# Mask products on GpSimd, quarter-array bias products and a new order of work in a fused attention and mixer kernel

## The chip, the core and the metric

The kernel runs on one core of a Trainium2 chip. A core has several engines that run side by side, each with its own queue: TensorE multiplies matrices (PE in the profile; its weight loads are PEld), VectorE (DVE) and ScalarE (ACT) work on elements, GpSimd (POOL) can do so too and issues transfers, and SyncE (SP) issues transfers. They wait for each other by semaphores. The metric is the device time of one execution in microseconds, as the median of several runs.

## What is computed

Attention over 4 images, 8 heads, 768 tokens and 64 numbers per head, in which a query sees 8 global keys and the last 96 tokens, with a bias that falls with the distance; then a mixer over the 512 numbers of each token.

```python
scores = scale * np.matmul(q, k.transpose(0, 1, 3, 2))
dist = np.where(is_global & ~is_local, float(n_local), np.abs(rel))
scores = np.where(keep, scores - slopes[:, None, None] * dist, -1e9)
a = np.exp(scores - max);  a = a / a.sum(-1)
x = np.matmul(a, v)                      # (4, 768, 512) after the heads are joined
xt = x.transpose(0, 2, 1)
u = x + (xt @ U @ V).transpose(0, 2, 1)  # rank 32, over the tokens
out = u + np.maximum(u @ w_ch1, 0.0) @ w_ch2   # 512 -> 2048 -> 512
```

Inputs and output are float32; the kernel multiplies in float16.

## The kernel before

**Staging.** Heads are taken in pairs, so there are 16 pairs p, four to an image. Everything is kept in SBUF; the eight PSUM banks (`ps`) take the products. q and k of a pair are loaded by GpSimd's queue and cast on the way (`lq`, `lk`; `add_load`, L491 to L547). There are two forms of load: pairs below `BP` are loaded by token, one transfer with long rows (L502), and the others by two transfers with rows of one head (L506). Pair 0 alone comes as float32 by SP's queue and is cast by ACT or VectorE (`Ck0`, `Cq0`, L413 and L411). q and k then have to be turned so that the head's numbers lie on the partitions: either by TensorE (`TK`, `TQ`; by-token loads with half-array products, `tr`, L629, others with full ones, `flip`, L648) and a copy out of PSUM (`EK`, `EQ`), or, for pairs in `QD`, by a transposing transfer on SP (L662).

**Attention.** A pair has three score groups s of two query blocks each. For the pairs of image 0 the bias and the mask come first as a product of a scaled identity `ib` with a table of distances `rel3` (`SB`, L758), and the scores are added to it in PSUM (`S`, L777, 64 rows to a product, two heads side by side). ACT takes the exponential (`EX`, L842). For the other images the exponential is multiplied by a precomputed factor instead (`MK`, L851 and L855, on VectorE, inputs `ep` and `mask`). Then come the product with v (`PV`, L912 and L913), the reciprocal of the sum and the normalizing (`RC`, `NM`, L951).

**Mixer.** The rank-32 part runs through `UP`, `XU`, `HM` (L896, L1025, L1007) and a sum into `uT` (`E0`, L1084, VectorE, which reads PSUM). The first big product, u times w_ch1, is done in eight units z for an image: either plainly (`M1a`, `M1b` with a relu on ACT, L1121 and L1145) or with seven products in place of eight (Strassen's way; `ZP1` to `ZP7`, L1215), whose partial sums ACT copies out of PSUM (`ZU`, `ZW`, `ZX`, L411) and VectorE adds (`ZA`, `ZB`, `ZD`, L1232). Before the change image 0 is plain, image 1 takes units 2 to 7 this way, images 2 and 3 all eight: 22. The second product is also done with seven (`RS`, L1310, and `P1` to `P7`, L1321), from sums of relu's results that VectorE makes (`Sa` to `Sd`, L1277), and VectorE adds the results to x (`DA` to `DH`, L1333, L1352, L1365). SP stores the rows (`O`, L1374).

**What sets the order.** Each step above is a named task. The list `ORDER` gives the order of all tasks by hand; a planner (L142) walks the list, gives out PSUM banks and buffers, estimates a start for each task by constants of its own, and the tasks are emitted by that start. So the order on each engine is fixed when the program is built, an engine does its tasks strictly one after the other, and a task that waits holds those behind it. `CFG` says by letter (A, D, P, S) which engine takes a copy of each pair. At the end of the kernel, `idle` (L1406) puts products of zeros into TensorE's queue: seven wide ones ahead of the first real product, and narrow ones into planned gaps of the first stretch.

Of the kernel before, what the change touches and what calls it, by code (L numbers as in the profile page):

```python
# [11 lines left out]
FP16 = mybir.dt.float16  # L12
I32 = mybir.dt.int32
AF = mybir.ActivationFunctionType
ALU = mybir.AluOpType
# [6 lines left out]
wz lk1 lk0 lq0 iota ones0 lk2 relf lq1 rel3 Ck0.1 Ck0.0 bias0 lv0 TK0 Cq0.1 Cq0.0 bias1 SB0.2 SB0.0 SB0.1 TQ0 EK0.1  # L22
lq2 EK0.0 KO0.1 bias2 mask0 bias4 EQ0.0 KO0.0 EQ0.1 TK1 EK1 S0.0 S0.2 S0.1 TQ1 EX0.0 mask4 TK2 SB1.2 KO1 EX0.1 SB1.1
ones1 EQ1 S1.2 lk3 lv1 VC0 VG0 EK2 EX0.2 S1.1 PV0 mask6 EX1.2 lq3 SB1.0 TQ2 ones3 TK3 EX1.1 EQ2 S1.0 RC0 NM0 KO2 VC1
VG1 ones2 vs1 lv2 vs0 SB2.0 SB2.2 S2.2 S2.0 EX1.0 TQ3 PV1 lv3 back XC0 EQ3 u16 w1_0 VC2 EX2.2 RC1 EK3 EX2.0 VG2 KO3
SB2.1 S2.1 NM1 VC3 XC1 SB3.1 SB3.0 S3.0 S3.1 EX2.1 EX3.0 PV2 mixl SB3.2 S3.2 EX3.1 RC2 NM2 VG3 EX3.2 XC2 UP0 UP1 XE1
lk4 PV3.0 PV3.1 XU1 lk5 PV3.2 TE1 HM1 E01 E00 RC3.0 RC3.2 TK4 RC3.1 NH3.0 NH3.2 NH3.1 UP2 UP3.0 UP3.1 UP3.2 EK4 w1_1
TK5 NM3 XE3 M1a0.0 XU3 TE3 mask2 EK5 M1c0.0 HM3 E03 w1_3 vz lq4 w1_2 w1_5 E13 M1a0.3 M1c0.3 M1a0.2 M1c0.2 E02 M1d0.2
M1d0.3 M1b0.2 M1d0.0 M1b0.0 M1b0.3 TQ4 RL0.2 RL0.0 KO4 M1a0.1 M1c0.1 M1d0.1 M1b0.1 RL0.3 EQ4 M1b0.4 M1a0.7 RL0.1 RM0.4
mask1 S4.1 RL0.7 S4.0 EX4.2 M1b0.5 M1b0.7 lv4 EX4.1 EX4.0 RM0.5 M1a0.5 M1a0.4 RL0.5 mask5 M1a0.6 M1b0.6 w1_4 RM0.6  # L30
RL0.6 RM0.7 mask3 lk7 lk6 w1_7 w1_6 w2_3 M1a0.15 MK4.2 TK6 vs2 w2_1 lq5 TK7 EK6 KO6 MK4.1 VC4 VG4 MK4.0 PV4 lq7 lq6
w2_2 lv5 w2_0 M1a0.10 M1b0.12 RL0.10 ZS1 RL0.4 M1a0.13 RL0.13 RM0.12 RC4 M1a0.9 NM4 TD0 Sa0.0 Sb0.0 KO5 Sc0.0 EK7
Sd0.0 TWa1 TWb1 M1b0.9 M1b0.15 M1b0.8 RM0.9 mask7 RL0.9 RL0.15 M1b0.13 M1b0.10 RM0.15 TQ5 EQ5 RM0.13 M1b0.11 RM0.8
RM0.11 M1b0.14 M1a0.12 M1a0.14 ZS2 RM0.10 RL0.12 RL0.14 RM0.14 M1a0.8 M1a0.11 RL0.8 RL0.11 lq8 lv6 S5.0 lk11 lv9 S5.1
lk10 Sa0.1 Sb0.1 EX5.0 lk8 RS0.1 Sd0.1 P20.1 lv7 EX5.1 TQ6 TQ7 MK5.1 MK5.0 TWa0 RS0.2 P20.2 P30.2 VC5 EQ7 EX5.2 EQ6
VG5 P10.1 S6.1 P50.1 P10.2 MK5.2 TWb0 DA0.1 KO7 DA0.2 EX6.2 PV5 EX6.1 S6.0 VC6 DF0.2 P60.2 EX6.0 VG6 RC5 NM5 XC5 XT5
EQ8 MK6.0 XC4 XT4 P30.1 S7.1 EX7.2 MK6.2 MK6.1 Sc0.1 DF0.1 EX7.1 P60.1 P50.2 PV6 S7.0 DB0.2 EX7.0 RS0.0 P10.0 UP5 UP4
RC6 DB0.1 MK7.1 P70.2 P20.0 MK7.0 NM6 MK7.2 VC7 VG7 DC0.2 PV7 DD0.2 P70.1 DA0.0 RC7 NM7 XC6 XE5 XU5 ZS3 P40.2 TE5
DG0.2 HM5 P60.0 DB0.0 XC7 P30.0 UP6 UP7 P50.0 VC9 XE7 XU7 EK8 E05 E04 DD0.1 EK10 TE7 DF0.0 XT6 XT7 P70.0 lk15 lq9 lq12
HM7 E06 DD0.0 E07 E17 ZT1 P40.1 ZP11.7 lk9 ZP11.6 M1a1.1 ZP21.7 M1b1.1 RL1.1 ZP11.4 P40.0 ZU1.6 ZP21.6 ZU1.4 ZP61.6  # L40
ZW1.6 lv8 DG0.0 lv10 ZU1.7 ZA1.6 DC0.0 ZP21.4 lq10 ZP61.4 ZP51.6 ZP71.6 ZP11.5 ZW1.4 ZP71.4 ZA1.4 KO8 ZA1.7 DG0.1
DC0.1 ZX1.6 ZX1.4 ZB1.6 ZP51.4 EQ12 M1b1.4 ZP61.7 ZP41.6 ZB1.4 ZU1.5 ZP21.5 ZP31.6 ZP41.4 ZP61.5 ZA1.5 KO10 ZR1.6
ZD1.6 ZP31.4 ZD1.4 O0.3 ZW1.7 O0.2 RM1.4 ZP71.7 ZR1.4 S8.1 ZW1.5 ZX1.7 ZP51.7 ZP71.5 ZP41.7 ZP51.5 ZB1.7 EX8.2 ZP31.7
ZX1.5 ZP41.5 ZB1.5 TD1 S8.0 ZP31.5 EX8.1 ZP11.3 ZR1.7 ZP11.2 EK9 EX8.0 ZP21.3 ZU1.3 ZD1.7 ZU1.2 ZR1.5 VC8 ZP21.2
M1a1.0 ZP61.2 MK8.2 MK8.1 ZD1.5 MK8.0 O0.5 EQ10 M1b1.0 ZP61.3 ZP51.3 ZW1.2 ZP51.2 O0.4 O0.1 O0.0 EQ9 Sa1.1 lk12 ZA1.3
# [1414 lines left out]
```

## Time and profile before

| what | value |
|---|---|
| median of 3 runs | 212.17 us (212.1 to 213.61) |
| profiled execution | 213.81 us, its span 211.9 us |
| TensorE busy | 204.9 us, 97% |
| VectorE busy | 180.5 us, 85% |
| ScalarE busy | 139.2 us, 66% |
| GpSimd busy | 74.2 us, 35% |
| moved by transfers | 27.40 MB |

The span runs from the first to the last instruction; some 1.9 us of the execution lie around it. Busy times are sums of an engine's instructions; a matrix product's duration contains its way through the array, so that a following product starts before the first has ended. A row of the groups names the line, the engine, the operation, the tiles (out<-in), the shape and count, then the busy time, the mean duration in ns, and the idle time just before with what ended it.

### The profile page before, as it was taken

The page shows a single profiled execution, that of the slowest core. Times are in us where ns is not written, and L with a number is a line of the kernel's source. Part 1 is how long each engine was busy: PE and PEld are TensorE (multiplying, and loading weights), DVE is VectorE, ACT ScalarE, POOL GpSimd, SP SyncE. Part 2 cuts the span into 40 slices and gives each one's busy share as a digit, 9 for nine tenths or more (in the row PEclk, how much of TensorE's full clock was granted, in tenths as well). Part 3 has the DMA queues.
Part 4 walks back from the last instruction along what each step waited for, and adds up shares of the span by engine and source line. Part 5 has one row for each costly group of instructions (what it writes and reads, how often), then busy time and mean ns, then how long its engine had stood idle before and what let it go on. Part 6 is the DMA issues. An engine that isn't in the chain of part 4 may idle for free.

```text
span 211.9 us, 5673 instructions
## 1 busy us (share of the span) xinstructions
PE 204.9 (97%) x2281; PEld 149.1 (70%) x2281; DVE 180.5 (85%) x369; ACT 139.2 (66%) x254; POOL 74.2 (35%) x98
## 2 busy tenths in 40 slices
PE   5999899999999999999999999999999999999992
PEld 1665756666888876556889866567889766668892
DVE  4389841999999999799999999899999996899872
ACT  4599869998999617899976366778783258740000
POOL 7699797647910494082755000003000000000000
PEclk9999999999999999999999999999999999999999
DMA  6999999999995899999999983866603110000644
GB/s 181 170 161 159 162 183 175 208 169 191 158 115 100 120 161 146 204 267 148 113 140 136 135 178 66 210 175 52 67 0 77 37 49 3 2 0 3 223 152 175
DMA packets 103643, 27.40 MB, mean 129 GB/s; under 512 B 91584, under 2 KB 100736, under 8 KB 103616
## 3 DMA queue, kind: packets, MB, share of 16 engines
q0 software_dynamic: 72192, 13.59, 83.7%
q1 hardware_dynamic: 31424, 13.45, 30.0%
q8 instruction: 18, 0.29, 0.6%
q14 instruction: 9, 0.07, 0.1%
HBM read 27.75 MB, written 6.29 MB: 161 GB/s over the span
## 4 chain that ended last, share of the span: by engine, by line
PE 86%; DVE 4%; DMA 3%; POOL 2%; issue 2%; POOLq 0%
PE ps L1321 36%; PE ps L1215 24%; PE ps L1121 6%; PE ps L777 5%; DMA w<-in_moe_w_ch_dram 3%; PE ps L758 3%; PE ps L913 3%; PE ps L912 2%; PE ps L1310 1%; PE ps L1145 1%; PE ps L648 1%; PE ps L629 1%; PE ps L896 1%; POOL stgk L506 1%; PE ps L1007 1%
## 5 line engine op out<-in xcount | busy, mean ns | idle before, releaser
L842 ACT ACTIVATE ep<-ps 128x1024 f16<-128x1024 f32 (+1 forms) x48 | 44.0, 955 | 6.9 <-PE ps L777 6.6
L1321 PEld LDWEIGHTS <-htr 128*128 128x128 f16 x392 | 35.8, 98 | 5.8 <-issue 0.5
L1321 PEld LDWEIGHTS <-sA 128*128 128x128 f16 x288 | 27.3, 98 | 4.2 <-issue 0.3
L506 POOL DMA_DIRECT2D stgk<-in_k_dram x24 | 20.2, 859 | 26.8 <-DMA kT<-stgk 26.7
L1333 DVE TENSOR_TENSOR x_sb<-x_sb,ps 128x256 f32<-128x256 f32 (+1 forms) x60 | 26.8, 463 | 3.1 <-PE ps L1321 2.6
L1232 DVE CUSTOM_DVE_ANT_0 htr<-ps,zu 128x384 f16<-128x384 f32 x50 | 26.0, 549 | 3.7 <-PE ps L1215 3.0
L411 ACT ACTIVATE zu<-ps 128x384 f32<-128x384 f32 x50 | 22.9, 497 | 6.6 <-PE ps L1215 4.4
L1215 PEld LDWEIGHTS <-w 128*128 128x128 f16 x176 | 17.0, 98 | 10.5
L1321 PE MATMUL ps<-w,sA 128*128 128x256 f16 x192 | 24.3, 273 | 0.0
L1321 PE MATMUL ps<-tB,htr 128*128 128x256 f16 (+1 forms) x200 | 24.1, 268 | 0.1
L1321 PE MATMUL ps<-w,htr 128*128 128x256 f16 x192 | 24.0, 273 | 0.0
L506 POOL DMA_DIRECT2D stgq<-in_q_dram x24 | 20.1, 860 | 2.9 <-PE ps L648 2.1
L1121 PE MATMUL ps<-uT,w 128*128 128x384 f16 x112 | 19.5, 326 | 0.0
L510 POOL DMA_DIRECT2D vt<-in_v_dram x16 | 16.6, 1043 | 7.5 <-ACT vo L411 3.7
L855 DVE TENSOR_TENSOR ep<-ep,mask 128x1024 f16<-128x1024 f16 x24 | 16.0, 682 | 3.6 <-ACT ep L842 3.6
L1215 PE MATMUL ps<-zt,w 128*128 128x384 f16 x88 | 19.0, 326 | 0.0
L1215 PE MATMUL ps<-uT,w 128*128 128x384 f16 x88 | 18.5, 326 | 0.0
L1121 PEld LDWEIGHTS <-w 128*128 128x128 f16 x112 | 10.8, 98 | 7.0
L951 DVE TENSOR_TENSOR x_sb<-ps,rcp 128x768 f32<-128x768 f32 x16 | 15.2, 952 | 0.3
L1215 PE MATMUL ps<-zt,zs 128*128 128x384 f16 x64 | 14.5, 326 | 0.0
L777 PE MATMUL ps<-qT,kT 64*128 64x128 f16 x192 | 14.1, 218 | 0.0
L913 PE MATMUL ps<-vt,ep 128*128 128x65 f16 x192 | 13.4, 193 | 0.3 <-DVE ep L851 0.3
(124 smaller groups left out, 397.8 us busy)
## 6 DMA issues: line engine op xcount, KB each, us to landing
out_dram<-x_sb SPq DMA_DIRECT2D x22, 256.0 KB, 2.6
vt<-in_v_dram POOLq DMA_DIRECT2D x16, 192.0 KB, 6.1
stgk<-in_k_dram POOLq DMA_DIRECT2D x24, 96.0 KB, 6.3
stgq<-in_q_dram POOLq DMA_DIRECT2D x24, 96.0 KB, 6.5
w<-in_moe_w_ch_dram POOLq DMA_DIRECT2D x8, 256.0 KB, 7.5
w<-in_moe_w_ch_dram POOLq DMA_DIRECT2D x4, 512.0 KB, 8.8
stgk<-in_k_dram POOLq DMA_DIRECT2D x3, 192.0 KB, 5.2
stgq<-in_q_dram POOLq DMA_DIRECT2D x3, 192.0 KB, 5.4
```

What stands on the lines that cost most here:

```text
L411: nc.scalar.activation(dst, src, AF.Copy)
L506: nc.gpsimd.dma_start(o[:, i], src[b, h0 + i].rearrange("(n p) d -> p n d", p=P))
L510: nc.gpsimd.dma_start(vt[gv.slot][:, :, :, 0:D], v[b, h0:h0 + 2].rearrange("h (n p) d -> p h n d", p=P),)
L777: nc.tensor.matmul(t[:, hi, j * P:(j + 1) * P], lhs, qt[r, i * P:(i + 1) * P], start=not biased, stop=True, skip_group_check=biased,)
L842: nc.scalar.activation(ep[gep.slot][:, :, lo:512], ps[:, gsc.slot:gsc.slot + 2, lo:512], AF.Exp, scale=qk_scale)
L855: nc.vector.tensor_tensor(ev, ev, mv, ALU.mult)
L913: nc.tensor.matmul(o, e[:, hi, (j + 1) * P:(j + 2) * P], vv[:, hi, i, 0:D1], start=(i == 0), stop=True)
L1121: nc.tensor.matmul(ps[:, g.slot, 0:HS], w1[:, dc, jt * P:(jt + 1) * P], ub[:, dc, i * HS:(i + 1) * HS], start=(dc == 0), stop=(dc == NDC - 1),
L1215: nc.tensor.matmul(bank(g), a()[:, i], bq[:, i], start=first and i == 0, stop=last and i == 1, skip_group_check=True,)
L1232: return lambda: nc.vector._custom_dve(TENSOR_ADD_SAT, out=o, in0=x(), in1=y(), s0=3.0e38, s1=0.0)
L1321: nc.tensor.matmul(o if part is None else o[:, part], a[:, j, c0 + cols.start:c0 + cols.stop], bq[:, j] if part is None else bq[:, j, part ...
L1333: nc.vector.tensor_tensor(o, o, x, ALU.add)
```

## The change

The same result is computed. The parts:

- Twelve of the 36 mask products (all of pair 8, one or two of pairs 9, 11, 12, 13, 14 and 15) run on GpSimd instead of VectorE.
- The bias products of pairs 1 to 3 are each split into two products of 64 rows and 64 columns (the scaled identity's off-diagonal blocks are zero). The two heads use opposite row halves, for which a copy of `rel3` with swapped halves (`rel3s`) is made, so that four products cover the four quarters of the array.
- Pairs 4 to 6 are now loaded by token (and turned by half-array products); pair 7 joins the pairs whose q and k are turned by transfers, nine in all.
- Image 1 takes all eight units of the first product with seven products: 24 units.
- For nine pairs the sum into `uT` no longer reads PSUM: ACT copies (`AH`) and VectorE adds in SBUF.
- Single copies change engines (`CFG`'s letters): both halves of pair 0's k are cast by ACT, two bias scalings go to VectorE, three pairs' values are copied by SP, one cast is no longer a transfer.
- Nine wide products of zeros lead instead of seven, and the narrow ones number 25 instead of 10.
- `ORDER` is new throughout. The planner's constants change, which tells in the emitted order and the count of zeros alone. A wider VectorE sum (`DX`) is added, with no pair that uses it, and an unused branch for `KG` goes.

```diff
-    "Z": [[1, [2, 3, 4, 5, 6, 7]], ...
+    "Z": [[1, [0, 1, 2, 3, 4, 5, 6, 7]], ...
-    "BP": 4,
+    "BP": 7,
-    "IB": "AAAA",  "C0": "ADDDDADA",
+    "IB": "AADD",  "C0": "AADDDADA",
-    "VO": "DDDDDAAAAAAADASA",  "XC": "DDADAAAAAAAAQAAA",
+    "VO": "DDDDDDAAASSADSDA",  "XC": "DDADAAAAAADAAAAA",
-    "QD": [8, 9, 10, 11, 12, 13, 14, 15],
-    "EA": (),
+    "QD": (7, 8, 9, 10, 11, 12, 13, 14, 15),
+    "EA": [4, 5, 6, 8, 9, 10, 12, 13, 14],
+    "SBQ": [1, 2, 3],
+    "MP": [24, 25, 26, 27, 35, 36, 38, 40, 43, 44, 45, 47],
...
+    def swap_rel():
+        for i in range(2):
+            nc.vector.tensor_copy(rel3s[64 * i:64 * i + 64], rel3[64 - 64 * i:128 - 64 * i])
...
                 for hi in range(2):
-                    bb = rel3[:, 128:384].unsqueeze(1).broadcast_to((P, 2, 256)) if s else rel3
-                    nc.tensor.matmul(t[:, hi, lo:512], ib[:, h0 + hi], bb, start=not by_glob, stop=by_glob, skip_group_check=True)
+                    if not quads:
+                        nc.tensor.matmul(t[:, hi, lo:512], ib[:, h0 + hi], cols(rel3, slice(0, P)), start=True, stop=False, skip_group_check=True)
+                        continue
+                    for i in range(2):
+                        o, r = slice(64 * i, 64 * i + 64), slice(64 * (i ^ hi), 64 * (i ^ hi) + 64)
+                        nc.tensor.matmul(
+                            t[o, hi, lo:512], ib[r, h0 + hi, r], cols(rel3s if hi else rel3, r), start=True, stop=False, skip_group_check=True,
+                        )
...
+            slow = 3 * p + s in CFG.get("MP", ())
+
-            def mk(s=s, gep=gep):
+            def mk(s=s, gep=gep, eng=nc.gpsimd if slow else nc.vector):
                 e = ep[gep.slot]
                 if s == 0:
-                    nc.vector.tensor_tensor(e[:, :, 128:512], e[:, :, 128:512], mask[:, h0:h0 + 2], ALU.mult)
+                    eng.tensor_tensor(e[:, :, 128:512], e[:, :, 128:512], mask[:, h0:h0 + 2], ALU.mult)
...
-    done, until = c_wz.end + 0.3, pl.names["M1a0.0"].start
+    done, until = 0.0, pl.names["M1a0.0"].start
...
+                bank = pl.unused("ps", done, t.start)
+                if not done:
+                    idle(9, 512, bank)
+                    done = pl.READY - 0.1
                 gap = t.start - done
-                bank = pl.unused("ps", done, t.start)
-                if bank is not None and done < 5.0:
-                    idle(int(gap / 0.43 + 0.6), 512, bank)
-                elif bank is not None and gap > 0.15:
+                if bank is not None and gap > 0.15:
                     idle(int((gap - 0.05) / 0.056), P, bank)
```

`AH` and its sum are in the kernel before already, unused (`EA` was empty):

```python
nc.scalar.activation(zu[gh.slot].bitcast(FP16)..., ps[:, gx.slot:gx.slot + 2, 0:HS], AF.Copy)   # AH
nc.vector.tensor_tensor(o, o, zu[gh.slot].bitcast(FP16), ALU.add)                             # E0, o = uT[b % 2][:, hp]
```

More of the change, by code (lines that the diff above doesn't have):

```diff
@@ L204, in run @@
             raise RuntimeError("order and tasks differ")
-        clock = {PE: 0.0, ACT: 2.0, DVE: 0.7, POOL: 0.75, SP: 0.7}
+        clock = {PE: self.READY, ACT: 2.0, DVE: 0.7, POOL: 0.75, SP: 0.7}
         last = {}
@@ L208, in run @@
         mode = 0
-        dma_free = {POOL: 0.0}
+        dma_free = {POOL: 0.0, SP: 0.0}
         shared_port = {POOL: [], DVE: []}
@@ L860, in attention @@
                 MK = add(
-                    DVE, 0.57 if s == 0 else 0.7, mk,
+                    POOL if slow else DVE, ((0.57, 0.7), (1.8, 2.35))[slow][s > 0], mk,
                     [EX, c_mask[h0], c_mask[h0 + 1]], fast=2, name=f"MK{p}.{s}",
```

207 lines of the change are left out of this document (111 added, 96 removed).

## The prediction

> **What bounds the kernel now.** I read the page first, then stretches of the span, then the chain, then the start by itself.
>
> ```profile
> span 211.9 us, 5673 instructions
> ...
> PE 204.9 (97%) x2281; PEld 149.1 (70%) x2281; DVE 180.5 (85%) x369; ACT 139.2 (66%) x254; POOL 74.2 (35%) x98
> ```
>
> ```profile
> 0.00:5.33 5.33, 3.17 (x7) 0.91 (x8) 2.46 (x12) 2.21 (x4) 4.27 (x12) 1.00 0.67 180
> 5.33:42.00 36.67, 35.52 (x476) 23.20 (x477) 22.81 (x57) 30.53 (x51) 30.20 (x41) 1.00 1.74 173
> 42.00:188.80 146.80, 146.78 (x1604) 107.87 (x1604) 138.53 (x265) 106.25 (x200) 39.75 (x46) 1.00 1.14 117
> ...
> 144.00:168.00 24.00, 24.00 (x343) 20.01 (x342) 23.41 (x42) 15.12 (x23) 1.83 (x2) 1.00 0.41 52
> ```
>
> After each stretch and its length stand the busy times of PE, PEld, DVE, ACT and POOL. From 42 us on, TensorE is busy for 146.78 of 146.80 us: there the time is the number of products, each at its own pitch, and nothing else. Two things qualify that. VectorE is busy 138.5 of the same 146.8 us, and 23.4 of 24 us while the last image's attention runs: it is the next bound. And up to 42 us TensorE has gaps (5.33 us until real work, 1.15 us after) and, as the start shows below, products at half pace. So I price three things: the products, the first 10 us, and whether anything makes TensorE wait after 42 us.
>
> **The products.** The chain gives the pitch of each kind (start, length, count), free of the drain that a product's own duration contains.
>
> ```profile
> 14.59 0.33 PE ps L758 x2
> 14.92 0.85 PE ps L629 x24
> ...
> 19.39 0.86 PE ps L758 x4
> ...
> 48.56 0.34 PE ps L648 x6
> ...
> 61.81 1.85 PE ps L1321 x16
> 63.66 0.55 PE ps L777 x16
> 64.21 1.85 PE ps L1321 x16
> ...
> 171.90 16.93 PE ps L1215 x104
> ...
> 189.60 17.16 PE ps L1321 x160
> ```
>
> So 384 columns take 0.163 us (16.93/104; a bias product 0.165), 512 take 0.215, 256 take 0.107, 128 take 0.057. Half-array products run two at a time: 24 of 128 columns took 0.85, against 12 x 0.057 = 0.68. A change of array shape costs time too: 16 score products (half the rows, two at a time) should take 16 x 0.028 = 0.45 and took 0.55; the 16 full products behind them should take 16 x 0.107 = 1.72 and took 1.85. That is about 0.12 per change of shape.
>
> 1. Bias products of pairs 1 to 3. Eighteen go (6 of 384, 12 of 512 columns: 6 x 0.165 + 12 x 0.215 = 3.57 us); 36 quarter-array ones come, in nine groups of four that cover the four quarters. No row here shows quarters. Halves run two at a time, by rows and by columns, so I take four at a time: 3 x 0.165 + 6 x 0.215 = 1.79. Net -1.78. Bounds: two at a time 0.0; one at a time +3.57; no gain beyond four, since the four columns' streams are the same length.
> 2. Units 0 and 1 of image 1 take 14 products instead of 16: -4 x 0.163 = -0.65. They add six ACT copies, six VectorE adds (row L1232 below, 0.549 each: +3.3 us) and two ACT relus against fewer relus; bounded with VectorE's account below.
> 3. Transposes. Pairs 4 to 6 turn by half-array products instead of full ones and pair 7 by the DMA queue: 48 full ones of 128 columns go (-2.74), 72 halves come (+2.02): -0.72. Pair 7's two DMA turns stand in SP's queue long before its scores: in the built order some 15 us of products lie between, and a turn lands in 3.4 us (row below). Nothing waits for it.
> 4. Changes of shape, counted in the built order: 77 before, 89 after, 12 x 0.12 = +1.44.
>
> Sum of the products: -1.78 - 0.65 - 0.72 + 1.44 = **-1.71 us**, on the path in full, because TensorE has no idle time to swallow it.
>
> **The start.**
>
> ```profile
> 0.89 3.17 PE L1408 MATMUL ps<-zero 128*128 128x512 f16 x7 [0.89 <-POOL zero L428]
> ...
> 3.79 0.52 ACT L411 ACTIVATE stgk<-sA 128x384 f16<-128x384 f32 x1 [1.77 <-DMA sA<-in_k_dram]
> ...
> 4.38 0.80 DVE L413 CAST stgk<-sA 128x384 f16<-128x384 f32 x1
> ...
> 5.33 0.80 PE L648 MATMUL ps<-ident,stgk 128*128 128x128 f16 x6 [1.27 <-DVE stgk L413]
> ...
> 5.73 0.63 DVE L413 CAST stgq<-sA 128x384 f16<-128x384 f32 x2 [0.54 <-DMA sA<-in_q_dram]
> ...
> 5.92 2.55 PE L758 MATMUL ps<-rel,ibe 128*128 128x512 f16 x6
> ...
> 8.27 0.85 PE L648 MATMUL ps<-ident,stgq 128*128 128x128 f16 x6
> 9.15 0.56 DVE L413 COPY qT<-ps 128x384 f16<-128x384 f16 x1 [2.80 <-PE ps L648]
> ...
> 9.83 0.29 PE L777 MATMUL ps<-qT,kT 64*128 64x128 f16 x2
> ...
> 11.63 0.50 PE L629 MATMUL ps<-ident,stgk 128*64 128x128 f16 x12
> ```
>
> Six bias products took 2.55 us where six at the later pitch would take 1.2 (4 x 0.215 + 2 x 0.165) and a drain of 0.2: until about 10 us TensorE runs at half its pace, although the granted clock prints 1.00 there. The seven products of zeros end at 4.06 and TensorE then idles 1.27 us, waiting for the half of k that VectorE casts behind its mask building (4.38 to 5.18). In the changed kernel ACT casts both halves (3.79 + 2 x 0.52 = 4.83, so TensorE starts near 4.95), and nine wide and five narrow products of zeros (9 x 0.43 + 5 x 0.107 = 4.4 us from 0.89) leave no pause. Then comes q's transpose: before, it stood behind the six bias products and started at 8.27 although q was cast at 6.36; now it starts at about 6.5, and 8.27 to 9.83 = 1.56 us later, at 8.1, the first scores can run. Two thirds of the bias products now stand between: behind a transpose at half pace (6.5 + 0.64) they take 1.5 at half pace (to 8.6) or 0.76 at full pace (to 7.9). So the first scores come 1.2 to 1.75 us earlier; I take **-1.4 us**. Bounds: 0 if ACT, busy 30.5 of 36.7 us here, holds the next stages; -2.2 if the clock is full throughout. ACT loses two bias scalings and the odd copy, so I lean to the gain.
>
> [...]
>
> **The mask products, and who waits.**
>
> ```profile
> L1232 DVE CUSTOM_DVE_ANT_0 htr<-ps,zu 128x384 f16<-128x384 f32 x50 | 26.0, 549 | 3.7 <-PE ps L1215 3.0 <-ACT zu L411 0.6 <-ACT htr L1260 0.2
> ...
> L855 DVE TENSOR_TENSOR ep<-ep,mask 128x1024 f16<-128x1024 f16 x24 | 16.0, 682 | 3.6 <-ACT ep L842 3.6
> ...
> L842 ACT ACTIVATE ep<-ps 128x768 f16<-128x768 f32 x16 | 13.0, 815 | 2.3 <-PE ps L777 2.1
> ...
> L1084 DVE TENSOR_TENSOR uT<-uT,ps 128x768 f16<-128x768 f16 x9 | 8.4, 948 | 0.0
> ...
> L851 DVE TENSOR_TENSOR ep<-ep,mask 128x768 f16<-128x768 f16 x12 | 6.6, 550 | 0.0
> ...
> L1174 DVE TENSOR_TENSOR zt<-uT,zt 128x768 f16<-128x768 f16 x3 | 1.7, 558 | 0.1
> ...
> L430 POOL IOTA ibe<- 128x256 int32 x1 | 0.4, 361 | 0.1
> ```
>
> VectorE loses 8 x 0.682 + 4 x 0.550 = 7.7 us of mask products and 9 x (0.948 - 0.558) = 3.5 us of sums that now read a copy made by ACT; it gains 3.3 (point 2) and some 2 to 3 us of small copies. Net near -5 us, so it does not become the bound by its own work. ACT's nine added copies (0.8 each) fall where it is 66% busy; they make those sums about 0.5 us later, behind which the order puts products of the image before.
>
> What a product costs GpSimd no row shows. From below: VectorE's 0.68. From above: writing 256 numbers took GpSimd 0.361, so 1024 take 1.44 in one pass and 2.9 if each of two inputs costs a pass. I take 2.2 (1.65 for 768), between one pass and two. [...] Who waits: TensorE, at the product with v behind each. Pairs 8 and 12 have 16 us or more of products in between. The tightest is pair 15's last: its scores, then 8 small and 24 products (0.3 + 24 x 0.107 = 2.9), then the product with v. The other way takes a drain 0.2, an exponential 0.815, the mask product 1.65 and two hand-overs of 0.1: 2.87. Even; but pair 13's cast (0.84) stands ahead of that exponential on ACT. In GpSimd's queue pair 15's value load sits between two mask products, which costs 1 us of POOL, not of TensorE. I put **+0.5 us** on all twelve; bounds 0 and 3 (0.75 late at each of pairs 11, 13, 14, 15 at 2.9).
>
> The rest hides: six fewer load issues on POOL and larger packets for pairs 4 to 6 lie off the path; values copied by SP instead of ACT land in 3 us with more than that in hand.
>
> **The end.**
>
> ```profile
> 208.33 0.42 DVE x_sb L1333
> ```
>
> ```profile
> out_dram<-x_sb SPq DMA_DIRECT2D x22, 256.0 KB, 2.6
> ...
> kT<-stgk SPq DMA_TRANSPOSE x8, 3.4
> ...
> out_dram<-x_sb SPq DMA_DIRECT2D x2, 64.0 KB, 2.1
> ```
>
> The last sum (0.42) and store (256 KB, 2.6) become a half-width sum, some 0.13 shorter, and 64 KB (2.1): **-0.5 us**, with 0 as bound if the larger stores just ahead hold the queue.
>
> **The sum.** -1.71 - 1.4 + 0.5 - 0.5 = -3.1 us. The profiled execution took 213.81 us (span 211.9 and 1.9 around it), so 210.7 beside it. It stands 1.64 over the median of the three runs; nothing in the kernel's rows explains that, so I carry the difference over: 212.17 - 3.1 = **209.0 us**.
>
> **Rivals.**
> A. [...] If VectorE's operations with both inputs in SBUF cannot run while GpSimd multiplies, then pairs 12 to 15, where VectorE is busy 23.4 of 24 us, pay: seven products there free 4.5 us, the three sums 1.2; if each stops VectorE for 1.8 us (midway between 0.68 and 2.9), 12.6 us come back, net of 5.7 and 0.6 us of slack 6.3 us on TensorE: 215.3. It is slower than before once a product stops VectorE for over (6.3 + 3.1)/7 = 1.35 us. For it: VectorE's load. Against it: half of VectorE's work reads PSUM, and no row has POOL stopping it. [...]
> B. *Quarters run two at a time*: point 1 gives nothing, 210.8. One at a time: 214.4.
> C. *The start is ACT's*: the early scores wait for exponentials and point "start" gives nothing: 210.4. For it: ACT's 30.5 of 36.7 us. Against it: the waits for the first scores are TensorE's own queue.
> D. *More is hidden in the start*: the 1.15 us of gaps up to 42 us also close, since loads of pairs 4 to 6 come in fewer packets, and the start gives 2.2: 207.
>
> **How the numbers follow.** Within 1% (210.05 to 214.3) is about what a measurement can't tell from no change. Forecast 0.55, A 0.15, B 0.11 (nearly all two at a time), C 0.12, D 0.07. Faster by over 1%: forecast and D, 0.62. Within: B, C and a mild A, 0.24. Slower: 0.14. The range runs from D with fuller bounds, 206.2, to A as far as its deciding point and a little short of its price, 213.2; above it lie most of A and B's far end, about 0.15.
>
> **What would show it.** The quarters' four products start within 0.01 us of each other and a group takes 0.215; first scores near 8.3 us; products at full pace before 8 us; POOL products of 1.65 to 2.2 us; TensorE busy without gaps at pairs 11 to 15; last store 64 KB. It is wrong if VectorE has idle time ended by POOL, or TensorE waits for POOL's products, or the groups of four take 0.43.

## The result and the profile after

The changed kernel takes **220.06 us** (median of 4 runs, 218.68 to 221.35) where the kernel before, on the same chip, takes 212.89 us (4 runs, 212.1 to 213.97). The ratio is 1.033, its 95% interval 1.025 to 1.042: slower, where 209.0 us was forecast. A median here takes in every run; a ratio leaves out the runs in which the core was in its slower state. The profiled execution took 218.68 us. Its page begins:

```profile
span 216.9 us, 5793 instructions
...
PE 204.0 (94%) x2336; PEld 147.7 (68%) x2336; DVE 186.0 (86%) x372; ACT 139.7 (64%) x253; POOL 91.7 (42%) x103
...
PEclk9999999999999996999999999999999999999998
```

TensorE's share fell from 97% to 94%, and one of the 40 slices shows the granted clock at 6 tenths. The same stretches that showed TensorE without a gap before now read as follows (start and end, length, busy time of PE, PEld, DVE, ACT, POOL, then the clock, the share of the DMA engines and GB/s):

```profile
78.00:90.00 12.00, 8.22 (x45) 4.64 (x44) 11.03 (x18) 5.42 (x12) 6.97 (x5) 0.86 1.71 152
90.00:126.00 36.00, 36.00 (x435) 27.13 (x433) 33.93 (x65) 24.86 (x45) 17.59 (x18) 1.00 1.12 133
126.00:144.00 18.00, 16.60 (x137) 10.46 (x136) 16.37 (x32) 13.66 (x29) 4.63 (x4) 1.00 1.08 196
144.00:168.00 24.00, 23.74 (x332) 19.04 (x331) 21.82 (x37) 16.60 (x28) 11.62 (x6) 1.00 0.31 43
```

Between 78 and 90 us TensorE idles 3.78 us, and the clock of 0.86 takes 0.14 x 12 = 1.7 us more; between 126 and 168 us it idles 1.66 us. That is 7.1 us, against nothing before; in the stretches left out here it is busy throughout, as before. The timeline around 80 us shows the first of these waits (start, duration, engine, line, tiles; in brackets the idle time ahead and what ended it):

```profile
75.68 1.70 POOL L520 DMA_DIRECT2D stgk<-in_k_dram  x2
76.46 5.09 DVE L1196 TENSOR_TENSOR zt<-uT 128x768 f16<-128x768 f16 x1
77.33 2.20 POOL L878 TENSOR_TENSOR ep<-ep,mask 128x1024 f16<-128x1024 f16 x1
79.42 1.70 POOL L874 TENSOR_TENSOR ep<-ep,mask 128x768 f16<-128x768 f16 x1
81.58 0.56 DVE L1197 TENSOR_TENSOR zt<-uT,zt 128x768 f16<-128x768 f16 x1
82.19 0.78 PE L1238 MATMUL ps<-zt,zs 128*128 128x384 f16 x2 [3.29 <-DVE zt L1197]
83.46 1.87 PE L1351 MATMUL ps<-tB,htr 128*128 128x256 f16 x8 [0.48 <-DVE x_sb L1363]
```

A sum of VectorE with both inputs in SBUF (L1196) takes 5.09 us where the next one of its kind takes 0.56. It ends at 81.55 us, 0.43 us after pair 8's second mask product on GpSimd. These sums are the operands of image 1's seven-product units, so TensorE waits 3.29 us for them, and then runs at half pace from 82.27 to 85.68 us by the trace's record of its clock, 3.41 us. Eight of L1351's products take 1.87 us in it (last row), where 16 take 1.92 at 75.03 us.

The second place is a copy of VectorE, beside pair 12's last mask product. It takes 2.18 us; the others of its shape in this trace take 0.31 to 0.63:

```profile
131.77 2.11 POOL L878 TENSOR_TENSOR ep<-ep,mask 128x1024 f16<-128x1024 f16 x1
131.90 2.18 DVE L421 COPY vo<-vt 128x660 f16<-128x660 f16 x1
134.00 1.01 DVE L1255 CUSTOM_DVE_ANT_0 htr<-ps,zu 128x384 f16<-128x384 f32 x2
134.59 0.48 PE L1238 MATMUL ps<-zt,w 128*128 128x384 f16 x2 [1.36 <-DVE htr L1255]
```

Now the account against the 5.0 us by which the span grew (211.9 to 216.9). If every product is counted with the pitch of its kind, the products come to 196.53 us before and 194.84 after: -1.69. What TensorE's first 42 us hold beside pitch fell from 10.66 to 9.45: -1.2. From 42 us on it rose from 0.7 to 8.2: +7.5, of which +5.5 between 78 and 90. The way from TensorE's last product to the end of the span grew from 3.65 to 4.17: +0.5. The sum is +5.1.

### The profile page after: what moved, and what is told of

Same layout as the page of the kernel before. It is cut to its first block, busy times and chain, and to the rows that moved or that the text cites. A ratio compares the mean times of both kernels' runs of the same rounds, so it can differ in the third digit from the quotient of the medians.

```text
span 216.9 us, 5793 instructions
## 1 busy us (share of the span) xinstructions
PE 204.0 (94%) x2336; PEld 147.7 (68%) x2336; DVE 186.0 (86%) x372; ACT 139.7 (64%) x253; POOL 91.7 (42%) x103
## 4 chain that ended last, share of the span: by engine, by line
PE 69%; DVE 21%; issue 4%; ACT 3%; POOL 1%; DVEq 0%; POOLq 0%
PE ps L1351 27%; PE ps L1238 22%; PE ps L1144 5%; PE ps L803 4%; PE ps L1168 3%; DVE x_sb L1363 2%; DVE zt L1196 2%; ACT ep L863 2%; PE ps L936 2%; DVE x_sb L974 2%; PE ps L935 2%; DVE sA L1307 2%; DVE ep L878 1%; PE ps L1340 1%; PE ps L642 1%
## 5 line engine op out<-in xcount | busy, mean ns | idle before, releaser
L1351 PEld LDWEIGHTS <-htr 128*128 128x128 f16 x392 | 36.4, 99 | 7.3 <-issue 1.7
L419 ACT ACTIVATE zu<-ps 128x384 f32<-128x384 f32 x56 | 26.2, 491 | 14.4 <-PE ps L1238 10.5
L1255 DVE CUSTOM_DVE_ANT_0 htr<-ps,zu 128x384 f16<-128x384 f32 x56 | 29.3, 552 | 5.3 <-PE ps L1238 3.3
L1351 PEld LDWEIGHTS <-sA 128*128 128x128 f16 x288 | 27.5, 98 | 3.6
L1238 PEld LDWEIGHTS <-w 128*128 128x128 f16 x192 | 18.6, 99 | 13.3 <-issue 1.8
L1351 PE MATMUL ps<-tB,htr 128*128 128x256 f16 (+1 forms) x200 | 25.0, 274 | 0.5 <-DVE x_sb L1363 0.5
L1351 PE MATMUL ps<-w,sA 128*128 128x256 f16 x192 | 24.3, 273 | 0.0
L878 POOL TENSOR_TENSOR ep<-ep,mask 128x1024 f16<-128x1024 f16 x8 | 17.7, 2214 | 15.2 <-ACT ep L863 15.2
L1351 PE MATMUL ps<-w,htr 128*128 128x256 f16 x192 | 23.5, 273 | 0.0
L520 POOL DMA_DIRECT2D stgk<-in_k_dram x18 | 15.1, 852 | 14.1 <-DMA kT<-stgk 9.8
L520 POOL DMA_DIRECT2D stgq<-in_q_dram x18 | 14.9, 844 | 13.3 <-DMA qT<-stgq 7.6
L1238 PE MATMUL ps<-zt,zs 128*128 128x384 f16 x72 | 17.1, 331 | 3.3 <-DVE zt L1197 3.3
L1238 PEld LDWEIGHTS <-zs 128*128 128x128 f16 x108 | 10.4, 98 | 10.4 <-DVE zt L1197 3.7
L419 ACT ACTIVATE x<-x_sb 128x768 f16<-128x768 f32 x12 | 10.2, 848 | 10.9 <-DVE x_sb L974 7.5
L874 POOL TENSOR_TENSOR ep<-ep,mask 128x768 f16<-128x768 f16 x4 | 6.6, 1656 | 17.6 <-ACT ep L863 17.6
```

Source lines behind the costliest of these rows:

```text
L419: nc.scalar.activation(dst, src, AF.Copy)
L520: nc.gpsimd.dma_start(o[:, i], src[b, h0 + i].rearrange("(n p) d -> p n d", p=P))
L878: eng.tensor_tensor(ev, ev, mv, ALU.mult)
L1238: nc.tensor.matmul(bank(g), a()[:, i], bq[:, i], start=first and i == 0, stop=last and i == 1, skip_group_check=True,)
L1255: return lambda: nc.vector._custom_dve(TENSOR_ADD_SAT, out=o, in0=x(), in1=y(), s0=3.0e38, s1=0.0)
L1351: nc.tensor.matmul(o if part is None else o[:, part], a[:, j, c0 + cols.start:c0 + cols.stop], bq[:, j] if part is None else bq[:, j, part ...
```

## The experiments

Mask products are numbered 3p + s by pair and score group; 24, 25 and 26 are pair 8's. "Kernel before" is always the one run on the same chip with the others. The medians of 7 to 19 such runs lay between 213.54 and 213.88 us.

**All twelve on VectorE.** The products are emitted on VectorE at their old places in the order; all else is the changed kernel.

```diff
-            def mk(s=s, gep=gep, eng=nc.gpsimd if slow else nc.vector):
+            def mk(s=s, gep=gep, eng=nc.gpsimd if slow and 3 * p + s not in (24, 25, 26, 27, 35, 36, 38, 40, 43, 44, 45, 47) else nc.vector):
```

> All twelve mask products are emitted on VectorE, each at its place in the order; every other instruction of the changed kernel, TensorE's order and the buffers stay. Theory (GpSimd's products stop VectorE's operations on SBUF): the three long stops go, 5.5 us at 78 to 86 us, 1.7 at 133, 0.5 at 149; 220.06 - 7.7 = 212.4, between 211 and 213.5, and VectorE's first difference of zt (L1196) of image 1 takes 0.55 us. Rival 1 (VectorE's own load is the bound): 7.7 us more on VectorE, so 220 or more. Rival 2 (zt came late because its inputs did, by the new route over ACT and the turning transfers): 219 to 221, with TensorE's gap of 3.5 us still there.

Measured: 216.67 us (216.25 to 218.25), ratio 1.016 (1.011 to 1.021); span 215.0. The long operations and the half-clock stretch are gone, and the loss fell from 3.3% to 1.6%, less than expected: about half of it is GpSimd's. The other half remained. The stretches show where:

```profile
78.00:90.00 12.00, 11.71 (x72) 6.89 (x71) 11.65 (x26) 9.53 (x22) 4.73 (x7) 1.00 1.73 184
90.00:126.00 36.00, 35.70 (x454) 27.42 (x453) 33.61 (x65) 23.82 (x42) 12.93 (x15) 1.00 1.48 140
126.00:144.00 18.00, 17.29 (x136) 9.90 (x135) 16.91 (x37) 14.09 (x30) 0.00 (x0) 1.00 1.03 190
144.00:168.00 24.00, 22.81 (x309) 18.49 (x307) 21.50 (x39) 14.13 (x23) 0.00 (x0) 1.00 0.18 34
```

In the kernel before, the first three of them read (the fourth stands in the prediction):

```profile
78.00:90.00 12.00, 12.00 (x91) 7.52 (x90) 10.38 (x23) 8.55 (x20) 3.85 (x5) 1.00 2.14 170
90.00:126.00 36.00, 36.00 (x460) 27.82 (x459) 35.48 (x67) 26.98 (x45) 15.54 (x18) 1.00 1.76 162
126.00:144.00 18.00, 18.00 (x133) 11.26 (x132) 16.67 (x37) 13.05 (x30) 0.00 (x0) 1.00 0.57 140
```

TensorE idles 2.5 us in small gaps, most of them ended by VectorE. The loss is larger than the idle time, because ahead of each gap the last product's way through the array counts as busy (on this run's page a product of 256 columns lasts 0.27 us, and yet 16 in a row take 1.92): by the distances between the starts of products, TensorE loses some 4.7 us more in these 90 us than in the kernel before. Yet VectorE is busy 83.7 of the 90 us, less than the 85.9 of the kernel before. So the sum of VectorE's work does not explain it. Two of the waits behind the gaps are for transposing transfers of x:

```profile
124.44 0.56 DVE L1097 TENSOR_TENSOR uT<-uT,zu 128x768 f16<-128x768 f16 x1 [1.00 <-DMA uT<-x]
162.18 0.84 ACT L419 ACTIVATE x<-x_sb 128x768 f16<-128x768 f32 x1 [3.89 <-DMA uT<-x]
```

The largest gap of TensorE, 0.65 us at 163.07, stands behind the second. For the rest, where VectorE's operations stand in the new order is what is left. That is inferred: no run moved them alone.

**Pair 8's first two on VectorE, and the same two moved later.** In one run products 24 and 25 go to VectorE. In the other all stay on GpSimd, and these two are moved behind a later load in GpSimd's queue.

```diff
+ eng=nc.gpsimd if slow and 3 * p + s not in (24, 25) else nc.vector     # first run
...
+ behind(["MK8.1", "MK8.0"], "lk11")                                      # second run
```

> Only the two products of pair 8 that ran on GpSimd from 77.3 to 81.1 us are emitted on VectorE (behind zt in its order); ten stay on GpSimd. Theory: the 5.5 us at 78 to 86 us go, the rest stays: 214.5, between 213.5 and 216. Rival 2 (zt's inputs are late) and rival 3 (the load issues that stand in GpSimd's queue just ahead stop VectorE): 219 to 221, zt's first difference still some 2 to 5 us long.

> All twelve stay on GpSimd; the two products of pair 8 are moved in its queue behind the next load of k (pair 11), which was issued at 84.5 us, so that they run beside the sums that read PSUM. Theory (it is the meeting with zt, not the engine): 214.5, between 213.5 and 216.5, as with the two on VectorE. Rival (a product on GpSimd is too dear wherever it stands): 218 or more.

Measured: 218.47 us (217.03 to 220.98), ratio 1.027 (1.020 to 1.035), and 222.86 us (222.15 to 223.56), ratio 1.044. Both missed, for one reason. The sum at L1196 is free again, but the stop went on to the next operation that stood beside a product. First the run with two on VectorE, then the one with two later:

```profile
84.87 1.64 POOL L520 DMA_DIRECT2D stgk<-in_k_dram  x2 [7.17 <-DMA kT<-stgk]
85.42 3.53 DVE L1220 TENSOR_TENSOR w<-w 128x512 f16<-128x512 f16 x1
86.52 2.14 POOL L878 TENSOR_TENSOR ep<-ep,mask 128x1024 f16<-128x1024 f16 x1
```

```profile
85.73 6.87 DVE L1220 TENSOR_TENSOR w<-w 128x512 f16<-128x512 f16 x1
86.50 2.15 POOL L878 TENSOR_TENSOR ep<-ep,mask 128x1024 f16<-128x1024 f16 x1
88.59 1.65 POOL L874 TENSOR_TENSOR ep<-ep,mask 128x768 f16<-128x768 f16 x1
90.18 2.13 POOL L878 TENSOR_TENSOR ep<-ep,mask 128x1024 f16<-128x1024 f16 x1
93.11 0.82 PE L1238 MATMUL ps<-zt,zs 128*128 128x384 f16 x2 [5.10 <-DVE zs L1221]
```

The same operation at L1220 takes 0.43 us undisturbed. It waits through one product in the first run and through all three in the second.

**GpSimd writes instead of multiplying.** Pair 8's first two products go to VectorE as above, and ten fills of `rel3s`, which is read no more by then, stand in their place in GpSimd's queue.

```diff
+            if t.name in ("MK8.1", "MK8.0"):
+                for _ in range(5):
+                    nc.gpsimd.memset(rel3s, 0.0)
```

> The two products of pair 8 are on VectorE as before; at their place in GpSimd's queue stand ten memsets of rel3s, which no later product reads, so GpSimd writes SBUF for some 2 to 5 us and reads nothing. If only GpSimd's reading stops VectorE's second input: zt's first difference takes 0.55 us and the time is that of the two on VectorE, 213 to 216. If any GpSimd work on SBUF stops it: zt takes 2 us or more and TensorE's gap is back, 217 to 220.

Measured, one execution: 218.35 us. The fills stop nothing; the four sums beside them take their 0.55 us each:

```profile
77.46 4.79 POOL L1460 MEMSET rel3s<- 128x384 f16 x10
78.15 0.55 DVE L1196 TENSOR_TENSOR zt<-uT 128x768 f16<-128x768 f16 x1
...
85.87 3.13 DVE L1318 TENSOR_TENSOR td<-tmp 128x128 f16<-128x128 f16 x1
86.76 2.15 POOL L878 TENSOR_TENSOR ep<-ep,mask 128x1024 f16<-128x1024 f16 x1
```

So it was not GpSimd's being busy, nor its writing, that stopped VectorE here; what the products do besides is to read. The time missed the expected 213 to 216 us, since the third product, still there, stopped a small difference (0.22 us as a rule) for 3.13. The copy of 2.18 us beside pair 12's product has one input, not two; no run had fills beside it, so whether reading matters there as well is open.

**The twelve products left out.** Neither engine does them, so the output lacks the bias and mask of those score groups.

```diff
-            t.fn()
+            if t.name not in ("MK8.0", "MK8.1", "MK8.2", "MK9.0", "MK11.2", "MK12.0", "MK12.2", "MK13.1", "MK14.1", "MK14.2", "MK15.0", "MK15.2"):
+                t.fn()
```

> The twelve mask products that the change gives to GpSimd are left out altogether, everything else is as in the changed kernel: it has the change's matrix products, start and order, but neither GpSimd's products nor their load on VectorE. Theory (all that was lost beyond the prediction's sum is GpSimd stopping VectorE, and, with the products on VectorE, VectorE's own load): no stop of over 0.5 us on VectorE, no half clock after 20 us, TensorE's last product 2.0 to 3.0 us earlier than in the kernel before, whose stores then cost 0.5 more than before: time 1.5 to 2.5 us under the kernel before (ratio 0.988 to 0.993). Rival (the new order itself makes TensorE wait between 78 and 170 us, whoever multiplies): TensorE still loses 3 us or more there, ratio 1.00 to 1.01.

Measured: 218.23 us for the profiled execution, then 217.43, 214.74 and 214.58; ratio 1.011 (1.002 to 1.021). By its ratio this is the rival's side: without the products and with 7.7 us less to do for VectorE, the new order is still not faster than the old. Between 78 and 168 us, though, TensorE idles only 1.8 us here, less than the 3 us of the rival, and none of it before 144 us. The trace names two waits that were hidden in the forecast, both for transfers:

```profile
63.24 1.40 ACT L419 ACTIVATE vo<-vt 128x660 f16<-128x660 f16 x2 [3.79 <-DMA vt<-in_v_dram]
65.60 0.22 PE L936 MATMUL ps<-vt,ep 128*128 128x65 f16 x2 [1.71 <-ACT ep L863]
```

```profile
145.14 0.96 DVE L974 TENSOR_TENSOR x_sb<-ps,rcp 128x768 f32<-128x768 f32 x1 [1.51 <-DMA out_dram<-x_sb]
146.15 0.81 PE L1238 MATMUL ps<-uT,w 128*128 128x384 f16 x4 [1.09 <-DVE x_sb L974]
```

In the first, ScalarE waits 3.79 us for pair 6's values, and the exponential that TensorE needs stands behind that copy; a half-clock stretch followed (the mean clock is 0.91 from 60 to 78 us, 1.00 in the same stretch of the kernel before). In the second, pair 12's normalizing waits until image 1's stores have read the buffer that it writes. In the changed kernel this second wait does not show: pair 12's products with v run at 144.9 us there instead of 142.5, with the stores issued at the same time.

**Eight on GpSimd; then image 2's stores ahead as well.** Products 24, 25, 26 and 38, those beside the long operations, go to VectorE. In the second run image 2's six stores also stand ahead of image 3's first in SP's queue.

```diff
+ eng=nc.gpsimd if slow and 3 * p + s not in (24, 25, 26, 38) else nc.vector
...
+ behind(["O2.0", "O2.1", "O2.2", "O2.3", "O2.4", "O2.5"], "DF3.2")       # second run
```

> Pair 8's three mask products and pair 12's last one go to VectorE, at the same places of the order; the eight others stay on GpSimd. Theory (these four are the products that stopped VectorE for long; the other eight stand beside operations that read PSUM): the 5.09 and 2.18 us operations are gone and nothing over 1.3 us takes their place, no half clock after 20 us, VectorE loses 2.6 us to the four products where it is busiest; time 0.5 to 2.5 us over the kernel before (ratio 1.002 to 1.012), below the kernel with all twelve on VectorE. Rival (the stops move on to whatever stands beside the next products, as they did twice): one stop of over 2 us remains, ratio over 1.015.

> As the run with eight products on GpSimd, and image 2's six stores stand ahead of the first store of image 3 in SP's queue, so that they go when their rows are done instead of from 206 us on. Theory (in the changed kernel the last 15 stores go together and the last one waits for the transfers ahead of it): the way from TensorE's last product to the end of the span falls from 4.2 to 3.5 us or less, time 0.5 to 1.2 us under the run with the stores as they were. Rival (the last sum and its own 64 KB store set the end, not the ones ahead): the same time within 0.3 us.

Measured: 217.20 us (216.35 to 220.69), ratio 1.018 (1.010 to 1.025), and 215.45 us (214.75 to 215.69), ratio 1.010 (1.005 to 1.016). In the first the stops moved on once more, now to pair 14's products, so the rival was right (the rows are of the second run, where it is the same):

```profile
139.69 4.54 POOL L878 TENSOR_TENSOR ep<-ep,mask 128x1024 f16<-128x1024 f16 x2 [11.62 <-ACT ep L863]
...
142.30 2.01 DVE L1318 TENSOR_TENSOR td<-tmp 128x128 f16<-128x128 f16 x1
...
144.83 0.48 PE L1238 MATMUL ps<-zt,w 128*128 128x384 f16 x2 [1.25 <-DVE htr L1255]
```

The stores did as expected. Where SP's stores began (start, time from the first to the last, count), in the changed kernel and in the run with the stores moved:

```profile
205.87 8.30 SPq L1407 DMA_DIRECT2D out_dram<-x_sb  x15
```

```profile
166.45 44.83 SPq L1407 DMA_DIRECT2D out_dram<-x_sb  x15
```

TensorE's last product ends at 210.45 and 210.41 us in the two runs, and the spans are 214.7 and 213.8: the end shrank from 4.2 to 3.3 us.

**Five, then three on GpSimd, stores ahead.** 40, 45 and 47 go to VectorE too, and then also 43 and 44 (pair 14's).

```diff
+ ... not in (24, 25, 26, 38, 40, 45, 47)              # five are left
+ ... not in (24, 25, 26, 38, 40, 43, 44, 45, 47)      # three are left
```

> The changed kernel with image 2's stores moved ahead and only five mask products left on GpSimd (pairs 9, 11, 12 and two of pair 14): pair 13's and pair 15's go to VectorE too, since the run with eight showed a 2.0 us stop beside pair 13's and a 1.6 us one beside pair 15's. Theory (each stop removed gives back TensorE's gap beside it): TensorE's gap of 1.4 us near 143 and the one of 0.8 near 162 shrink; 0.8 to 2 us under the run with eight and the stores moved, so within 0.5 us of the kernel before. Rival (VectorE is full there, its own three products cost as much as the stops): the same as the run with eight, ratio 1.008 to 1.013.

> The changed kernel with image 2's stores moved ahead and only three mask products left on GpSimd (pair 9's first, pair 11's last, pair 12's first), the others on VectorE. Theory (the stop of 2.0 us beside pair 14's products was the largest loss left, 1.4 us on TensorE): no operation of VectorE is stretched by over 0.5 us after 75 us, TensorE's gap near 143 us is below 0.5; 0.5 to 1.5 us under the run with five. Rival (VectorE, with nine more products, is then late by itself): TensorE's gaps only spread, the time is that of the run with five within 0.5 us.

Measured: 215.84 us (215.25 to 221.44), ratio 1.013 (1.008 to 1.017), and 215.04 us (214.53 to 218.98), ratio 1.008 (1.005 to 1.012). With five the 2.0 us stop was unchanged, since pair 14's products caused it and not pair 13's, which the expectation had named; three products on VectorE gave nothing. With three no such operation is left after 75 us. The median is 0.8 us lower, as the theory has it, but the two intervals overlap, so that gain is not shown. The profiled execution (218.98) had the late values of pair 6 again; the stretch of the last image's attention still shows what stays:

```profile
144.00:168.00 24.00, 22.34 (x316) 17.54 (x315) 22.01 (x40) 15.46 (x25) 0.00 (x0) 1.00 0.18 31
```

TensorE idles 1.7 us there, where GpSimd has nothing to do at all and VectorE is busy 22.0 of 24 us, against 23.4 in the kernel before. Of this, 0.90 us stand behind ScalarE's copy of x, which waits 4.14 us for the same transposing transfer as in the run with all twelve on VectorE; the runs with eight and with five show that wait too, with 3.9 to 4.2 us.

**Full bias products in the changed kernel.**

```diff
-            def sbias(s=s, gsc=gsc, lo=lo, quads=quads):
+            def sbias(s=s, gsc=gsc, lo=lo, quads=False):
```

> The bias products of pairs 1 to 3 are full again (18 in place of 36 quarters), at the same places; all else is as in the changed kernel. Prediction's step (the quarters save 1.78 us on TensorE's path): the first big product starts 1.5 to 2.0 us later than in the changed kernel and TensorE's product 112 of the first big product too. Rival (the start is ScalarE's or the loads', the gain is given back): it starts later by less than 1 us, or the 112th product does.

Measured, one execution: 219.45 us. The first big product (`M1`, L1168) starts at 27.63 instead of 26.34 us, 1.3 later, and its 112th at 51.14 instead of 49.85. The sum of the pitches is 196.39 instead of 194.84: the quarters save 1.55 us of products and 1.3 on the path, less than the 1.78 forecast, and they lay between the two expectations. The time itself lies among those of the changed kernel.

**Parts of the change in the old order.** Three kernels keep the order, loads and engines of before. The first has the leading zeros alone (nine wide and eight narrow ones in place of seven), the second also the quarter products, the third the zeros and the twelve mask products on GpSimd. All three also copy the swapped table on VectorE, which the second alone reads.

```diff
-                    idle(int(gap / 0.43 + 0.6), 512, bank)
+                    idle(9, 512, bank)
...
+    "SBQ": [1, 2, 3],                                                     # second
...
+ eng=nc.gpsimd if 3 * p + s in (24, 25, 26, 27, 35, 36, 38, 40, 43, 44, 45, 47) else nc.vector   # third
```

> The kernel before with the leading products of zeros alone changed: nine wide and eight narrow ones in place of seven wide ones, five more narrow ones later in the start, and the copy of the swapped table on VectorE that nothing reads. Bias products full, all mask products on VectorE, order and loads of before. Theory (the start's term is real: TensorE reaches full pace by 5 us rather than 10, and what it saves stays, because nothing behind it is slower): at 42 us TensorE is 1.5 to 2.0 us ahead, and the time is 1.0 to 2.0 us under the kernel before (ratio 0.990 to 0.995). Rival (the loads and transposing transfers are a second chain as long as TensorE's, so that a gain in the start turns into a wait for a transfer, as it did with the quarters): TensorE waits for a transfer between 60 and 110 us, time within 0.5 us of the kernel before or above it.

> The order, the loads and the engines of the kernel before, with two parts of the change alone: the quarter-array bias products of pairs 1 to 3 and the nine leading products of zeros (eight narrow ones behind them). The copy of the swapped table stands on VectorE ahead of pair 1's first copy out of PSUM. Theory (the products' part of the prediction is right and is lost only to the waits that the new order and GpSimd bring later): nothing that waits after 42 us is changed, so what TensorE saves before 42 us stays to the end; 1.0 to 2.2 us under the kernel before (ratio 0.990 to 0.995). Rival (the early stretch is bound by ScalarE or VectorE, so that shorter products only turn into waits): within 0.5 us of the kernel before.

> The order, the loads and the engines of the kernel before, with the twelve mask products on GpSimd alone (and the leading zeros of the run beside it; full bias products). Theory (GpSimd's products stop whatever operation of VectorE with both inputs in SBUF stands beside them, wherever they are put): VectorE shows at least two operations of over 1.5 us after 75 us, TensorE's gaps with them; 2 to 6 us over the kernel before (ratio 1.01 to 1.03). Rival (the stops are an accident of the new order, in which loads stand just ahead of the products): no such operation, VectorE freed of 7.7 us, time within 1 us of the kernel before.

Measured: zeros alone 212.69 us (212.05 to 214.64), ratio 0.997 (0.994 to 1.000). With quarters 216.64 us (215.79 to 217.96), ratio 1.017 (1.009 to 1.025). With GpSimd's products 224.16 us (223.33 to 224.74), ratio 1.051 (1.044 to 1.058).

The third confirms the theory in an order that was never made for it, and costs more there than expected. Its worst place is at the products of pairs 13 and 14:

```profile
149.92 8.00 POOL L877 TENSOR_TENSOR ep<-ep,mask 128x1024 f16<-128x1024 f16 x3 [0.68 <-ACT ep L862]
...
153.07 2.88 DVE L1306 TENSOR_TENSOR sA<-sA,htr 128x1536 f16<-128x1536 f16 x1
155.87 3.73 DVE L1306 TENSOR_TENSOR sA<-htr,sA 128x1536 f16<-128x1536 f16 x2
...
159.66 0.61 PE L1350 MATMUL ps<-w,sA 128*128 128x256 f16 x2 [3.78 <-DVE sA L1306]
```

The second missed both expectations, the theory's by 4 to 5 us. TensorE stayed ahead until 90 us, then one wait took more than all that had been gained:

```profile
102.19 0.23 PE L802 MATMUL ps<-qT,kT 64*128 64x128 f16 x2 [3.29 <-DMA qT<-stgq]
```

Pair 9's scores wait for q's transposing transfer. In the kernel before, the two turns of q issued at 87.28 and 90.87 us; here, although TensorE is ahead, at 90.30 and 93.31, because a load that began at 71.62 us there begins at 72.61 here. Loads wait for buffers that the turns free, turns wait for loads, so the transfers form a chain of their own. Why that chain ran 1 to 3 us later in this run is not settled.

The first kernel is the only one at or under the time of before, by 0.3% with an interval that just reaches no change; more was expected. At 42 us its profiled execution was only 0.15 us ahead, while the run with GpSimd's products, identical up to there, was 1.95 us ahead. The trace's record of the granted clock turns to full at 6.79 us in the one and at 4.40 in the other, so the gain of a longer lead of zeros varies from execution to execution. What sets the moment, 2.39 us apart in these two, is not shown. After 78 us that execution lost 0.7 us, and there its rival was right: TensorE waits 0.55 us at 80.31 for VectorE's sum into `uT` (L1080), which itself had waited 0.65 us for the transposing transfer of x.

It is well ahead of the changed kernel; ahead of the one before it is not by more than the measurement can tell.

## Why the prediction was wrong

- **The products, -1.71 us: right.** The pitches sum to -1.69. The quarters run four at a time, as the rows below of the changed kernel show (four products start within 0.01 us, and the next four 0.21 later, the pitch of one full product of 512 columns). Their -1.78 was -1.55, and -1.3 on the path: a group that stands ahead of products of another shape takes 0.29 to 0.39 us until these begin.

```profile
18.28 0.40 PE L781 MATMUL ps<-rel,ibe 64*64 64x512 f16 x2
18.29 0.40 PE L781 MATMUL ps<-rel3s,ibe 64*64 64x512 f16 x2
18.49 0.40 PE L781 MATMUL ps<-rel,ibe 64*64 64x512 f16 x2
18.52 0.38 PE L781 MATMUL ps<-rel3s,ibe 64*64 64x512 f16 x2
```

- **The start, -1.4 us: right in place, 1.2 in size.** The first scores run at 8.33 us (8.3 forecast), the clock is full at 3.8. The zeros alone gave 0.15 to 1.95 us by 42 us, and nine other executions with the changed kernel's start were between 0.06 us ahead of it and 0.6 behind at 42 us, so a part of this term is luck of the execution.
- **"+0.5 us on all twelve": this step failed.** The durations it rests on were right:

```profile
L878 POOL TENSOR_TENSOR ep<-ep,mask 128x1024 f16<-128x1024 f16 x8 | 17.7, 2214 | 15.2 <-ACT ep L863 15.2
L874 POOL TENSOR_TENSOR ep<-ep,mask 128x768 f16<-128x768 f16 x4 | 6.6, 1656 | 17.6 <-ACT ep L863 17.6
```

  But it priced only the products with v behind each mask product, and there TensorE waits for none of them. What they cost is VectorE's stops: 3.29 and 0.48 us of waiting, the 1.7 us of half clock that follow, and 1.36 at pair 12. The sign that was named for it, idle time of VectorE ended by GpSimd, could not show it: a stopped operation counts as busy. With the products on VectorE the ratio is 1.016 instead of 1.033. The forecast's ratio was 0.985: of the 4.8% that it missed by, 1.7 go with these products, and 3.1 stay without them and belong to the steps below.
- **Rival A had the mechanism at the wrong place and price.** It put the stops at pairs 12 to 15 with 1.8 us each, and so came to 215.3 us. The worst stop stands at pair 8: the stopped operation makes the operands with which TensorE goes on, two products follow each other without an opening, and the slowed clock comes on top. Its chance of 0.15 was set by "no row has POOL stopping it"; no row of before could have, as GpSimd multiplied nothing there. "Half of VectorE's work reads PSUM" was right (55% of the summed time of its operations in the kernel before), and such operations were not stretched: in the changed kernel the 13 of L1255 that lie beside a product take 0.54 to 0.56 us, as the 59 others do.
- **"It does not become the bound by its own work": right by the sum, wrong in what was made of it.** With the twelve products on VectorE it is less busy than before, yet with all stops gone TensorE idles 2.5 us between 78 and 168 us and loses some 4.7. The forecast carried "TensorE busy for 146.78 of 146.80 us" over to an order in which every engine's queue is new. That this step failed is shown. Of the causes, late transposing transfers are seen behind some of the gaps, the largest among them; what makes the others stays open.
- **"The rest hides": true of the profiled execution, but without a margin.** It was said of loads, turns and copies. In the changed kernel's trace TensorE has no gap between 42 and 78 us and waits for no transfer after. But pair 6's values came late in executions of two experiments in the new order, and stores of image 1 held pair 12's normalizing in one; and with the stops gone or fewer, ScalarE waits 3.9 to 4.2 us for a turn of x in the last image in six runs, TensorE 0.46 to 0.90 behind it. In the old order, with the quarters, q's turn held pair 9. Without any of the twelve products the new order is at 214.6 us at best, no faster than before.
- **The end, -0.5 us: failed; it was +0.5.** The bound of 0 for "the larger stores just ahead" was too kind: image 2's stores had been put behind image 3's first, and 15 stores left together at 205.87 us. Moving them shortened the end by 0.9 us.

## What to carry to other kernels

Moving two-input work to GpSimd was not free relief for VectorE here: a sum with both inputs in SBUF took 5.09 us in place of 0.56 beside two moved products, while L1255, which reads PSUM, kept its 0.54 to 0.56. So look at what VectorE does beside each moved product, and move it where those operations read PSUM. Look at the durations, not at idle time: a stopped operation is only longer, as L1220 was with 6.87 us in place of 0.43. If one stop is mended by shifting a product, look at what stands beside its new place. In a kernel whose bound engine has no idle time, a saved microsecond counts only once the next chain, here the transfers and the places of VectorE's small operations, has been shown to have slack.

## What was not expected of the hardware

- The stopped operation waited from before the product's recorded start. The sum at L1196 began at 76.46 and should have ended at 77.02, yet the product is recorded from 77.33; L1220 began at 85.42 with 0.43 to do, its product at 86.52. So VectorE was held at least 0.3 and 0.67 us ahead of the record, while GpSimd's issue of a load stood just ahead. The issue alone did not hold it: in the kernel before, 56 operations of VectorE with both inputs in SBUF overlap such issues, and none takes over 0.01 us longer than its kind does elsewhere. Whether the product begins earlier than recorded, or an issue holds VectorE when a product follows it, is not known.
- The two sums that had begun ahead of the first product were held through all that followed: 5.09 us over two, 6.87 over three. In the old order VectorE did get in between: operations begun during one product end at 153.15 and 155.95 us, 0.4 and 0.8 after a product's end at 152.74 and 155.13. The three products there took 2.4 to 2.8 us, where the changed kernel's eight took 2.1 to 2.5.
- The price of a pause of TensorE did not follow from its length. The wait of 3.29 us in the changed kernel was followed by 3.41 us of half clock, the one of 5.10 us in the run with two products moved later by some 6.9 (a mean clock of 0.77 from 84 to 99 us), and the wait of 3.29 us in the old order with quarters by none (1.00 from 90 to 108 us). In the traces of the two kernels full clock lasts 201.39, 78.51 and 129.71 us, which is 59, 23 and 38 times 3.413. If the busy time of TensorE is counted in steps of that length from the start of full clock, half clock followed the steps with 0.12, 0.12 and 0.77 us of work (the first from 78.86 to 82.27 us in the changed kernel, the two others at the end of a run), and none of the others, which held 2.25 us or more. For the old order an estimate: its mean clock of 0.998 over 214.5 us leaves some 0.9 us of half clock, all of it at the end, and counted back from there in the same steps the wait (98.90 to 102.19 us) fell across two, with some 1.3 and 2.2 us of work.
